# Attention and routed experts in one kernel: the remaining logits on VectorE, phase 0's last sum moved, a second bank for one turning, and a copied register

## The chip, the cores and the metric

The kernel runs as one program on one core of a Trainium2 chip. The metric is its time on the device in microseconds. Before the change three runs took 688.2, 688.75 and 691.17 us; the median is 688.75.

## The reference

The first half is attention with a window: 8 batches, 8 heads, 576 positions, 64 columns a head, all in float32. The second half sends each of the 4608 resulting rows `x` (512 columns) to one of 8 experts, by an assignment that is greedy over all rows and experts at once:

```
logits = x @ w_gate
for idx in argsort(-logits.flatten()):
    tok, e = idx // 8, idx % 8
    if assigned[tok] >= 0 or counts[e] >= 576: continue
    assigned[tok] = e; counts[e] += 1
for e in range(8):
    out[assigned == e] = relu(x[assigned == e] @ w1[e]) @ w2[e]
```

Each expert gets exactly 576 rows. `w1` has 512 x 1024 and `w2` 1024 x 512 elements an expert.

## The kernel before, in words

**Attention** fills about the first 203 us and leaves `x` in DRAM and the logits in SBUF (`L_sb`, 128 partitions, 8 experts, 36 columns).

**The router** (class `Router`) doesn't sort. It works in phases 0 to 7, and each phase settles one expert, the one that fills up next: it finds by counting which rows are its members, lists their numbers, and takes the expert and its rows out of the logits. In `few` (line 966) VectorE writes indicators `ind`, TensorE counts them (line 611), VectorE turns the counts to flags `sat` (line 625), and TensorE sums these over partitions (line 628). Then `T1` marks the members (line 911), `totals` (line 865) gives the counts `Dc` and the expert's key `mx`, `members` (line 708) makes `m`, its running sum `run` and the exclusive sum `ex` (lines 712 to 716), and TensorE makes positions of `ex` (line 723). From these come `loOH` (line 750), the small matmuls of line 759, and the row numbers `idx`. `later` (line 938) writes the logits that remain, `L1`: a penalty for full experts is added (`L2`), and another for the members. In phases 0 and 1 VectorE does that with two operations; from phase 2 on GpSimd does it with three (lines 949, 954, 955). The next phase's first choice reads `L1` (line 514).

**The experts** (class `MoE`) are computed one after the other, expert k beside the router's work on the next ones. SyncE reads the expert's number from SBUF into a register (`value_load`, line 1069) and loads its weights in pieces of 512 KB into four buffers `raw`. ScalarE casts each to a high part (line 1084) and VectorE subtracts to get the low part (line 1090). GpSimd gathers the expert's rows, five tiles `g`, with indirect DMAs (line 1106). Each tile is turned by `flip` (line 1116): four transposes by TensorE into one PSUM bank, a cast to `xh` by ScalarE, and `under`, VectorE's subtraction that gives `xl`. The bank of pool `ps_g` is the only one there; the last turnings of the first expert may use pool `ps_o`. Pool `ps_h` has four banks, for layer 1's sums. Layer 1 (line 1155) and layer 2 (lines 1199 to 1202) take three products of high and low parts. GpSimd scatters the results to `out` (line 1211).

**What sets the order.** In `first_expert` and in layer 2 of the first expert the engines TensorE, VectorE and ScalarE are wrapped in `OrderedCore` (line 470): they run in the order in which the program is written. There the generator `phase0` stands for the router, and each `go()` runs it to its next `yield`. Line 467 is the wrapper's, so that all instructions of that part carry it. `keep_warm(n)` (line 1111) issues `n` matmuls of zeros, 128 x 512, that nothing reads. Their numbers are in `ZEROS` and, inside `phase0`, in `ZEROS_0`. Around the end of phase 0 `first_expert` reads as below; the first `go()` is the last count, `go(2)` the flags `sat` and their sum, and the last one goes from `sel` over the members to their positions:

```
    m.low(W[0], raw[0], 1)
    go()
    a0 = m.flip(*ga[0], "o")
    m.keep_warm(ZEROS[2])
    go(2)
    m.low(W[1], raw[1], 0)
    a1 = m.flip(*ga[1])
    m.keep_warm(ZEROS[3])
    go()
```

In layer 2 of the first expert a counter `i` goes through the steps, and at `i` in `TURN_2` the next tile of the second expert is turned. From layer 1 of the second expert on, a planner at compile time orders each engine's instructions: among those that its own model of the times takes to be ready, it picks by the program's order. So an engine can have instructions in its queue that the program writes much later, and once queued they are run strictly in that order. `W_LOAD` and `W_SPLIT` say at which step a piece of weights is asked for and split. `m.marked` (line 1075) makes a copy of a register tile on VectorE; a load that reads the copy can't start before it. It is used for some loads of the first two experts.

Of the kernel before, what the change touches and what calls it, by code (L numbers as in the profile page):

```python
# [5 lines left out]
F32 = mybir.dt.float32  # L6
# [4 lines left out]
ALU = mybir.AluOpType  # L11
# [8 lines left out]
NT = N // 128  # L20
# [5 lines left out]
def attention(tc, pools, qk_in, v_in, rel_in, C, x_dram, L_sb, router):  # L26
# [292 lines left out]
    for n in range(NPAIRS + LAG + 2):  # L319
# [16 lines left out]
        if turns:  # L336
            ps = {}
            for t in (2, 1, 3):
                ps[t] = bank()
                turn(k, t, ps[t])  # L340
            turned(k, 2, ps[2], nc.scalar.copy)
# [15 lines left out]
        if turns:  # L357
            ps = bank()
            turn(k, 0, ps)
        if n < NPAIRS:  # L360
            scores(n, 0)
        if turns:
            turn(k, 4, ps)
            turned(k, 0, ps, nc.scalar.copy)
# [55 lines left out]
CONST_AT = 4  # L420
WARM, WARM0, WARM1 = 11, 16, 4
AHEAD = 18, 24, 24
ZEROS = 2, 4, 2, 3, 3
ZEROS_0 = 10, 2, 5, 8
CHOICE_1 = 1, 4
HIGHS_2 = 0, 3, 4, 5
LOWS_2 = 0, 0, 0, 2, 1, 2, 2, 1
# [3 lines left out]
CHOICE_2 = 25, 27, 31  # L431
SPLIT_2 = 26, 29
LATE_2 = 34
TURN_2 = 34, 36, 39
TURN_1, SPLIT_1, WAIT_1, SPLIT_W2, FLAGS_1 = (1, 2), (5, 6), 3, 8, 6
W_LOAD = [(0, 1, 0, 0), (0, 1, 1, 2), (0, 1, 2, 6), (0, 1, 3, 10),
          (1, 0, 0, 13), (1, 0, 1, 16), (1, 0, 2, 19), (1, 0, 3, 22), (1, 1, 0, 28)]
# [5 lines left out]
BIG = 1e30  # L443
# [12 lines left out]
def bc(ap, shape):  # L456
    return ap.to_broadcast(shape)
# [17 lines left out]
class Router:  # L475
# [462 lines left out]
    def later(self, k, L, T1, Dc, keyv, mx):  # L938

        nc, rt = self.nc, self.p["rt"]  # L940
        if k < 7:
            self.pen = self.small("pen", 8)
            nc.vector.tensor_scalar(self.pen, Dc, float(CAP), -BIG, ALU.is_ge, ALU.mult)
            self.base = self.small("base", 8)
            nc.vector.tensor_tensor(self.base, self.pen, Dc, ALU.add)
            nc.vector.scalar_tensor_tensor(self.left, keyv, mx[:, 0:1], self.left, ALU.not_equal, ALU.mult)
            L2 = rt.tile([128, 8, NT], F32, name="L2", bufs=1)
            eng = nc.vector if k < 2 else self.tc.nc.gpsimd
            eng.tensor_tensor(L2, L, bc(self.pen.unsqueeze(2), [128, 8, NT]), ALU.add)
            if k < 2:  # L950
                nc.vector.scalar_tensor_tensor(self.L1, T1, 100.0 * BIG, L2, ALU.mult, ALU.add)
            else:
                Lt = rt.tile([128, 8, NT], F32, name="Lt", bufs=1)
                eng.tensor_scalar(Lt, T1, 100.0 * BIG, 1.0, ALU.mult, ALU.mult)
                eng.tensor_tensor(self.L1, Lt, L2, ALU.add)

    def excess(self, Dc, mx):

# [102 lines left out]
class MoE:  # L1061
# [54 lines left out]
    def flip(self, h, g, r, pool="g"):  # L1116

        if h == 0:
            self.xg = [self.p["xg"].tile([128, 4, CAP], F32R, name=name) for name in ("xh", "xl")]
        if pool == "g":  # L1120
            ps = self.p["ps_g"].tile([128, 4, 128], F32, name="pg")
        else:
            ps = self.p["ps_o"].tile([128, 512], F32, name="po").rearrange("p (j t) -> p j t", j=4)
        for j in range(4):
            self.nc.tensor.transpose(ps[:, j, :r], g[:r, 128 * j:128 * j + 128], self.C["ident"][:r, :r])  # L1125
        self.nc.scalar.copy(self.xg[0][:, :, 128 * h:128 * h + r], ps[:, :, :r])  # L1126
        return h, r, ps
# [3 lines left out]
        xh, xl = (x[:, :, 128 * h:128 * h + r] for x in self.xg)  # L1131
        return self.nc.vector.tensor_tensor(xl, ps[:, :, :r], xh.bitcast(F32), ALU.subtract)  # L1132

    def turn(self, gs):

        for h, g, r in gs:
            yield self.under(*self.flip(h, g, r))

    def hidden(self):

# [121 lines left out]
def first_expert(tc, P, C, r, m, route):  # L1262

    nc = tc.nc
    r.nc = core = OrderedCore(tc)
    core.sync = nc.sync
    m.nc = core
    m.idle = P["ps_g"].tile([128, 512], F32, name="pg")
    p = r.phase0(lambda i: m.keep_warm(ZEROS_0[i]))

    def go(n=1):
        for _ in range(n):
            next(p)

    def ask(reg, layer, cs):
        return list(m.loads(reg, layer, cs))

    def marked(i):
        return m.marked(r.guess, i)

    cut = 0, AHEAD_ROWS, 576
    pp = {}

    def layer(f, t):
        for _ in m.steps1(W, f, cut, (t,), f < 2 and t == 0):
            pass
        pp[f, t] = m.pp

    def rest(f, t):
        m.rest1(pp[f, t], f, cut, (t,))  # L1290

    go()
    raw = ask(r.guess, 0, range(3))
    rows = [r.few_rows[:, t:t + 1] for t in range(2)]
    ga = m.gather(rows, range(2), m.x[0:128 * AHEAD_COLS, :])
    m.idle = P["ps_h"].tile([128, 512], F32, name="ph")
    W = [m.high(raw[c]) for c in range(2)]
    go(2)
    m.keep_warm(ZEROS[0])
    go(2)  # L1300
    m.low(W[0], raw[0], 0)
    m.keep_warm(ZEROS[1])
    go()
    m.low(W[0], raw[0], 1)
    go()
    a0 = m.flip(*ga[0], "o")
    m.keep_warm(ZEROS[2])
    go(2)
    m.low(W[1], raw[1], 0)
    a1 = m.flip(*ga[1])  # L1310
    m.keep_warm(ZEROS[3])
    go()
    m.under(*a0)
    m.under(*a1)
    late = marked(0)
    raw += ask(late, 0, (3,))
    second = ask(late, 1, (0,))
    m.keep_warm(ZEROS[4])
    m.hidden()
    go()  # L1320
    layer(0, 0)
    m.low(W[1], raw[1], 1)
    layer(1, 0)
    W.append(m.high(raw[2]))
    go()
    gb = m.gather(r.idx[0], range(2, 5))
    rest(0, 0)
    go()
    for half in range(2):
        m.low(W[2], raw[2], half)  # L1330
    layer(2, 0)
    W.append(m.high(raw[3]))
    rest(1, 0)
    layer(3, 0)
    go()
    rest(2, 0)
    layer(4, 0)
    for half in range(2):
        m.low(W[3], raw[3], half)
    rest(3, 0)  # L1340
    layer(5, 0)
    rest(4, 0)
    b = m.flip(*gb[0], "o")
    m.under(*b)
    late = marked(1)
    second += ask(late, 1, range(1, 4))
    layer(6, 0)
    rest(5, 0)
    b = [m.flip(*gb[1], "o"), m.flip(*gb[2])]
    m.under(*b[0])  # L1350
    rest(6, 0)
    m.under(*b[1])
    layer(7, 0)
    rest(7, 0)
    V, lows = [], []
    for f in range(8):
        layer(f, 1)
        if f == 0:
            go()
        if f in HIGHS_2:  # L1360
            V.append(m.high(second[len(V)]))
            lows += [(V[-1], second[len(V) - 1], half) for half in range(2)]
        if f:
            rest(f - 1, 1)
        if f in CHOICE_1:
            next(route)
        for _ in range(LOWS_2[f]):
            m.low(*lows.pop(0))
    rest(7, 1)
    next(route)  # L1370
    return V, p


def layer_moe(tc, P, C, r, m, exact):
    nc = tc.nc
    route = (n for k in range(1, E) for n in r.phase(k, exact))
    st = dict(wait=0, turn=0)
    raws, loaders, gathers = {}, {}, {}
    W = {}

    def load(e, layer):
        if (e, layer) not in loaders:
            loaders[e, layer] = m.loads(r.ei[e], layer)
            raws[e, layer], W[e, layer] = [], []
        raws[e, layer].append(next(loaders[e, layer]))

    def part(e, layer):
        W[e, layer].append(m.split(raws[e, layer][len(W[e, layer])]))
# [34 lines left out]
    if exact:  # L1423
        r.start(True)
        W[0, 0] = [m.split(raw) for raw in m.loads(r.ei[0], 0)]
        for _ in m.turn(m.gather(r.idx[0])):
            pass
        for _ in m.layer1(W.pop((0, 0))):
            pass
        V = [m.split(raw) for raw in m.loads(r.ei[0], 1)]  # L1430
        while 1 not in r.idx:
            next(route)
    else:
        V, p = first_expert(tc, P, C, r, m, route)
    i = 0
    for _ in m.layer2(V, m.h, r.idx[0], fine=True):
        i += 1
        if i in ROUTE_2 + CHOICE_2 and not exact:
            next(route)
        if i == ROUTE_2[-1]:  # L1440
            gathers[0] = m.turn(m.gather(r.idx[1]))
        if i == LOAD_2:
            raws[1, 0], W[1, 0] = list(m.loads(r.ei[1], 0, range(2))), []
        if i in SPLIT_2:
            part(1, 0)
        if i in TURN_2:
            turned = next(gathers[0])
        if i == LATE_2:
            late = m.marked(r.ei[1], 2)
            raws[1, 0] += m.loads(late, 0, (2, 3))  # L1450
            loaders[1, 1] = m.loads(late, 1)
            raws[1, 1], W[1, 1] = [], []
        if i == TURN_2[-1] and not exact:
            next(route)
# [55 lines left out]
def moe_attn_kernel(tc, qk, v, w1, w2, wn, rel, ident, cst, out):  # L1510
    nc = tc.nc
    with ExitStack() as es:
# [24 lines left out]
        for k, b in (("ps_g", 1), ("ps_h", 4), ("ps_o", 2)):  # L1537
            P[k] = es.enter_context(tc.tile_pool(name=k, bufs=b, space=PSUM))
        layer_moe(tc, P, C, r, m, False)
        again = P["rs"].tile([1, 1], I32, name="again")  # L1540
        nc.vector.tensor_copy(again, r.flag[0:1, 0:1])
        go = nc.values_load(again[0:1, 0:1], min_val=0, max_val=1)
        with tc.If(go > 0):
            r.nc = m.nc = nc
            layer_moe(tc, P, C, r, m, True)
# [26 lines left out]
```

## Time and profile before

| | |
|---|---|
| Median of three runs | 688.75 us |
| Profiled execution | 690.12 us, its span 688.2 us |
| TensorE busy | 97% of the span, 7299 matmuls |
| VectorE, ScalarE, GpSimd busy | 67%, 48%, 22% |
| Mean granted TensorE clock | 0.993 of full |
| Chain that ended last | PE 86%, DVE 7%, ACT 2%, DMA 2% of the span |

In the profile PE is TensorE, PEld its weight loads, DVE VectorE, ACT ScalarE, POOL GpSimd and SP SyncE. The span goes from the first to the last instruction; the execution's time is 1.92 us longer, and the profiled execution was 1.37 us above the median. In a timeline, the number in square brackets is how long the engine was idle before the instruction, with what released it. A matmul's duration includes its way through the array, so that durations of successive ones overlap.

### The profile page before, as it was taken

The numbers are of one execution on the slowest core, as the hardware profiler recorded it, in microseconds if no ns is written. First come the engines' busy times: TensorE is split into PE (matmuls) and PEld (weight loads), VectorE is DVE, ScalarE is ACT, GpSimd is POOL, SyncE is SP. The second block draws the span as 40 slices with busy tenths as digits, with TensorE's granted clock in tenths as the row PEclk, the third lists the DMA queues.
The fourth block names the chain that finished last, engine by engine and source line by source line (L and its number), as shares of the span: only waits on it lengthen the run. The fifth ranks groups of instructions, "written<-read, shape, count | busy, mean of one in ns | idle before, by whom it ended". The sixth has DMA issues, their size and how long they took to land.

```text
span 688.2 us, 18927 instructions
## 1 busy us (share of the span) xinstructions
PE 666.3 (97%) x7299; PEld 581.9 (85%) x7299; DVE 459.0 (67%) x1888; ACT 327.8 (48%) x992; POOL 149.4 (22%) x334
## 2 busy tenths in 40 slices
PE   8999999999996999999999999999999999999996
PEld 5899889989983996898798889879979988988985
DVE  6678888887878786799579377566746937423210
ACT  6898998898862441344414323322522524322201
POOL 4022222222121101304102311411311323111011
PEclk9999999999999999999999999999999999999999
DMA  8466575757324402626404503611810546401001
GB/s 297 156 199 214 183 232 172 217 179 227 119 86 147 156 36 93 222 70 217 158 9 158 201 25 123 208 47 31 290 48 24 184 162 199 155 31 38 1 25 50
DMA packets 35139, 92.72 MB, mean 135 GB/s; under 512 B 3808, under 2 KB 13152, under 8 KB 35040
## 3 DMA queue, kind: packets, MB, share of 16 engines
q1 hardware_dynamic: 29152, 72.55, 31.8%
q0 software_dynamic: 5888, 18.88, 8.4%
q8 instruction: 59, 0.97, 0.6%
q14 instruction: 40, 0.33, 0.2%
HBM read 72.54 MB, written 18.87 MB: 133 GB/s over the span
## 4 chain that ended last, share of the span: by engine, by line
PE 86%; DVE 7%; ACT 2%; DMA 2%; issue 1%; POOL 0%; POOLq 0%; SPq 0%; DVEq 0%; ACTq 0%
PE ph L1155 25%; PE po L1199 9%; PE po L1200 8%; PE pt L53 7%; PE po L1202 7%; PE x L53 6%; PE s L53 6%; PE pt L160 6%; PE ph L467 4%; PE po L467 2%; PE pg L1125 2%; ACT u L147 2%; DMA raw<-in_w_dram 1%; DMA g<-x,idxa 1%; PE x L1507 1%
## 5 line engine op out<-in xcount | busy, mean ns | idle before, releaser
L1155 PE MATMUL ph<-xh,hl 128*128 128x288 f32 x896 | 166.2, 299 | 0.0
L1155 PEld LDWEIGHTS ph<-xh,hl 128*128 128x128 f32 x896 | 134.6, 188 | 1.2 <-DVE hlo L1171 0.4
L147 ACT ACTIVATE u<-u,mn 128x192 f32<-128x192 f32 (+2 forms) x288 | 124.1, 439 | 5.5 <-DVE mn L137 5.4
L1199 PE MATMUL po<-hl,hh 128*128 128x512 f32 (+1 forms) x288 | 114.9, 399 | 0.0
L1200 PE MATMUL po<-hl,hh 128*128 128x512 f32 (+1 forms) x288 | 110.8, 385 | 0.0
L1155 PE MATMUL ph<-xl,hl 128*128 128x288 f32 x448 | 99.1, 296 | 0.0
L1160 ACT ACTIVATE hh<-ph 128x288 fp32r<-128x288 f32 x112 | 40.5, 408 | 120.0 <-PE ph L1155 117.8
L137 DVE CUSTOM_DVE_ANT_0 u<-s,bm 128x192 f32<-128x192 f32 (+1 forms) x248 | 71.8, 345 | 32.0 <-PE s L53 31.5
L1202 PE MATMUL po<-hl,hlo 128*128 128x512 f32 (+1 forms) x232 | 89.0, 384 | 0.0
L1211 POOL DMA_INDIRECT out_dram<-o,idx x38 | 41.4, 1090 | 204.5 <-ACT o L1206 81.2
L1090 DVE TENSOR_TENSOR hl<-raw,hl 128x512 fp32r<-128x512 f32 x108 | 70.5, 684 | 12.9 <-ACT hl L1084 12.3
L1084 ACT CAST hl<-raw 128x1024 fp32r<-128x1024 f32 x54 | 56.2, 1050 | 40.6 <-DMA raw<-in_w_dram 35.4
L1155 PEld LDWEIGHTS ph<-xl,hl 128*128 128x128 f32 x448 | 73.1, 188 | 0.1
L1199 PEld LDWEIGHTS po<-hl,hh 128*128 128x128 f32 x288 | 54.2, 188 | 10.1 <-issue 0.6
L1171 DVE SCALAR_TENSOR_TENSOR hlo<-ph,hh 128x288 fp32r<-128x288 f32 (+1 forms) x112 | 42.6, 416 | 29.5 <-ACT hh L1160 26.7
L1200 PEld LDWEIGHTS po<-hl,hh 128*128 128x128 f32 x288 | 54.3, 189 | 9.1
L53 PE MATMUL s<-qk 64*64 64x192 f32 (+1 forms) x992 | 60.6, 328 | 0.4 <-DVE mn L137 0.3
L1132 DVE TENSOR_TENSOR xl<-pg,xh 128x512 fp32r<-128x512 f32 (+1 forms) x32 | 20.2, 631 | 57.9 <-ACT xh L1126 57.8
L147 ACT ACTIVATION_READ_ACCUMULATOR u<-u,mn 128x1 f32 x288 | 56.3, 195 | 0.0
L1106 POOL DMA_INDIRECT g<-x,idx x38 | 40.4, 1063 | 68.4 <-issue 47.2
L160 PE MATMUL pt<-ident_sb,u 128*128 128x128 f32 x368 | 53.0, 280 | 0.5 <-ACT u L147 0.4
L1202 PEld LDWEIGHTS po<-hl,hlo 128*128 128x128 f32 x232 | 43.6, 188 | 8.9
(310 smaller groups left out, 1092.9 us busy)
## 6 DMA issues: line engine op xcount, KB each, us to landing
raw<-in_w_dram SPq DMA_DIRECT2D x64, 512.0 KB, 4.0
qk<-in_qk_dram SPq DMA_DIRECT2D x32, 576.0 KB, 5.6
v<-in_v_dram SPq DMA_DIRECT2D x32, 288.0 KB, 3.0
x<-xb SPq DMA_DIRECT2D x14, 512.0 KB, 4.1
x<-xb SPq DMA_DIRECT2D x8, 128.0 KB, 3.4
x<-xb SPq DMA_DIRECT2D x4, 256.0 KB
g<-x,idx POOLq DMA_INDIRECT x38, 6.2
out_dram<-o,idx POOLq DMA_INDIRECT x38, 2.7
```

The costliest lines, as they stand in the source:

```text
L53: put(nc.tensor.matmul(out, w, a, start=start, stop=stop, skip_group_check=True))
L137: put(nc.vector.tensor_tensor_reduce(out=weights(n, t, h), in0=x[:, c:c + 64 * m].rearrange("q (j k) -> q j k", k=64), in1=bm[n % NP][:, y ...
L147: put(nc.scalar.activation(u, u, AF.Exp, bias=st["mn"][:, i:i + 1], scale=-1.0, accum_out=st["sm"][:, i:i + 1]))
L160: put(nc.tensor.transpose(ps[:, c:c + 128], u[:, o + 128 * j:o + 128 * j + 128], ident))
L1084: self.nc.scalar.copy(hl[:, 0, :], raw)
L1090: self.nc.vector.tensor_tensor(hl[:, 1, c:c + 512], raw[:, c:c + 512], hl[:, 0, c:c + 512].bitcast(F32), ALU.subtract)
L1155: self.nc.tensor.matmul(pp[t], w[:, a, j, fo:fo + 128], x[:, j, cut[t]:cut[t + 1]], start=(i == 0), stop=(i == 11))
L1171: self.nc.vector.scalar_tensor_tensor(d, pp[t][:, c0:c1], 0.0, o[:, c0:c1].bitcast(F32), ALU.max, ALU.subtract)
L1199: nc.tensor.matmul(out, a, wh, start=(f == 0), stop=False)
L1200: nc.tensor.matmul(out, a, wl, start=False, stop=(f == 7 and t == 4))
L1202: nc.tensor.matmul(out, hl[:, f, 128 * t:128 * t + 128], wh, start=False, stop=(f == 7))
L1211: self.sent = self.tc.nc.gpsimd.indirect_dma_start(out=self.out, out_offset=bass.IndirectOffsetOnAxis(ap=idx[t][:r], axis=0), in_=o[:r, :] ...
```

## The change

`later` uses VectorE's two operations in all phases. In `first_expert`, the last count's flags and their sum come ahead of both turnings, and the numbers of fillers change. The second expert's second tile is turned through a bank of `ps_h`, and its third tile one step sooner. The loads of layer 2 of the third expert read a copied register.

```
-ZEROS = 2, 4, 2, 3, 3
-ZEROS_0 = 10, 2, 5, 8
+ZEROS = 2, 8, 3, 1, 1
+ZEROS_0 = 14, 2, 5, 9
-TURN_2 = 34, 36, 39
+TURN_2 = 34, 36, 38
...
-            eng = nc.vector if k < 2 else self.tc.nc.gpsimd
-            eng.tensor_tensor(L2, L, bc(self.pen.unsqueeze(2), [128, 8, NT]), ALU.add)
-            if k < 2:
-                nc.vector.scalar_tensor_tensor(self.L1, T1, 100.0 * BIG, L2, ALU.mult, ALU.add)
-            else:
-                Lt = rt.tile([128, 8, NT], F32, name="Lt", bufs=1)
-                eng.tensor_scalar(Lt, T1, 100.0 * BIG, 1.0, ALU.mult, ALU.mult)
-                eng.tensor_tensor(self.L1, Lt, L2, ALU.add)
+            nc.vector.tensor_tensor(L2, L, bc(self.pen.unsqueeze(2), [128, 8, NT]), ALU.add)
+            nc.vector.scalar_tensor_tensor(self.L1, T1, 100.0 * BIG, L2, ALU.mult, ALU.add)
...
-        if pool == "g":
-            ps = self.p["ps_g"].tile([128, 4, 128], F32, name="pg")
-        else:
-            ps = self.p["ps_o"].tile([128, 512], F32, name="po").rearrange("p (j t) -> p j t", j=4)
+        ps = self.p["ps_" + pool].tile([128, 512], F32, name="p" + pool).rearrange("p (j t) -> p j t", j=4)
...
-    def turn(self, gs):
+    def turn(self, gs, pools="ggggg"):
...
-            yield self.under(*self.flip(h, g, r))
+            yield self.under(*self.flip(h, g, r, pools[h]))
...
+    m.keep_warm(ZEROS[2])
+    go()
+    m.low(W[1], raw[1], 0)
+    go()
     a0 = m.flip(*ga[0], "o")
-    m.keep_warm(ZEROS[2])
-    go(2)
-    m.low(W[1], raw[1], 0)
     a1 = m.flip(*ga[1])
     m.keep_warm(ZEROS[3])
     go()
...
-            loaders[e, layer] = m.loads(r.ei[e], layer)
+            loaders[e, layer] = m.loads(m.marked(r.ei[e], 3) if (e, layer) == (2, 1) else r.ei[e], layer)
...
-            gathers[0] = m.turn(m.gather(r.idx[1]))
+            gathers[0] = m.turn(m.gather(r.idx[1]), "ghggg")
```

## Rows read from the trace of the kernel before

**Rows 1.** The page, busy time of each engine: us (share of the span) x instructions.

```profile
PE 666.3 (97%) x7299; PEld 581.9 (85%) x7299; DVE 459.0 (67%) x1888; ACT 327.8 (48%) x992; POOL 149.4 (22%) x334
```

**Rows 2.** Timeline of PE, 219 to 228 us: start, duration, operation, [idle before].

```profile
220.33 0.66 PE L467 MATMUL po<-ident_sb,g 128*128 128x128 f32 x4 [0.61 <-DMA g<-x,idxa]
...
221.51 0.18 PE L467 MATMUL m<-sat,c_ones 64*128 64x1 bf16 x1
...
222.53 1.49 PE L467 MATMUL ph<-zero 128*128 128x512 bf16 x3
...
224.68 1.30 PE L467 MATMUL ph<-xh,hl 128*128 128x256 f32 x8
...
227.74 0.41 PE L467 MATMUL m<-mv,loOH 128*128 128x24 bf16 x10
```

**Rows 3.** Timeline of DVE, 219 to 228 us.

```profile
220.33 0.15 DVE L467 TENSOR_SCALAR sat<-mx 64x1 bf16<-64x1 f32 x1
...
221.73 0.25 DVE L467 TENSOR_SCALAR sel<-kq,m 128x36 bf16<-128x36 bf16 x1 [0.63 <-PE m L467]
...
225.47 1.42 DVE L467 TENSOR_TENSOR loOH<-c_i,slo 128x1152 bf16<-128x1152 bf16 x2
```

**Rows 4.** Windows of half a microsecond: PE, PEld, DVE, ACT, POOL, clock, DMA.

```profile
221.00:221.50 0.50, 0.50 (x2) 0.00 (x0) 0.10 (x1) 0.48 (x1) 0.00 (x0) 0.63 0.00 0
224.50:225.00 0.50, 0.50 (x5) 0.32 (x3) 0.43 (x3) 0.00 (x0) 0.00 (x0) 0.96 0.00 0
```

**Rows 5.** Timeline of all engines, 280 to 286 us.

```profile
281.47 0.69 DVE L467 TENSOR_TENSOR xl<-pg,xh 128x512 fp32r<-128x512 f32 x1 [0.87 <-issue]
...
282.22 0.66 PE L467 MATMUL pg<-ident_sb,g 128*128 128x128 f32 x4 [0.48 <-DVE late L467]
```

**Rows 6.** Timeline of all engines, 325 to 333 us.

```profile
329.43 1.05 ACT L1084 CAST hl<-raw 128x1024 fp32r<-128x1024 f32 x1 [2.45 <-DMA raw<-in_w_dram]
...
332.23 0.66 PE L1125 MATMUL pg<-ident_sb,g 128*128 128x128 f32 x4 [1.22 <-DVE xl L1132]
```

**Rows 7.** Timeline of SP, 320 to 330 us: loads issued, with count.

```profile
321.01 5.04 SPq L1072 DMA_DIRECT2D raw<-in_w_dram  x4
```

**Rows 8.** Timeline of all engines, 364.5 to 368 us, one of four such stretches.

```profile
365.23 0.67 POOL L949 TENSOR_TENSOR L<-L,pen 128x288 f32<-128x288 f32 x1 [1.91 <-DVE ov L961]
...
365.38 0.56 DVE L712 SCALAR_TENSOR_TENSOR m<-am,kmx,sel 128x36 bf16<-128x36 bf16 x1
...
365.97 0.85 POOL L955 TENSOR_TENSOR L<-Lt,L 128x288 f32<-128x288 f32 x1
...
366.06 0.85 DVE L714 TENSOR_TENSOR_SCAN run<-c_ones,m 128x36 bf16<-128x36 bf16 x1
...
367.67 0.19 PE L723 MATMUL m<-ex,c_ones 128*128 128x36 bf16 x1 [0.79 <-DVE ex L716]
```

**Rows 9.** Waits, whole run: us in total, times, longest.

```profile
PE m L467 <- DVE ind L467: 3.7, 4, 1.6
...
PE m L723 <- DVE ex L716: 3.2, 4, 0.8
```

**Rows 10.** Groups of DVE, phases 0 and 1: busy us, mean ns | idle before.

```profile
L467 DVE SCALAR_TENSOR_TENSOR L<-T,L 128x288 f32<-128x288 bf16 x2 | 0.9, 458 | 0.1
...
L467 DVE TENSOR_TENSOR_SCAN run<-c_ones,m 128x36 bf16<-128x36 bf16 (+1 forms) x3 | 0.7, 227 | 0.1
...
L467 DVE TENSOR_TENSOR L<-L,pen 128x288 f32<-128x288 f32 x1 | 0.5, 451 | 0.0
...
L467 DVE SCALAR_TENSOR_TENSOR m<-am,kmx,sel 128x36 bf16<-128x36 bf16 x1 | 0.2, 245 | 0.0
```

**Rows 11.** The page, costliest groups: the gathers of GpSimd.

```profile
L1106 POOL DMA_INDIRECT g<-x,idx x38 | 40.4, 1063 | 68.4 <-issue 47.2
```

**Rows 12.** Line 1090 on DVE: min/median/max ns, first and last start.

```profile
L1090 DVE TENSOR_TENSOR hl<-raw,hl x108: 670/681/736, 298.9 to 631.7; 128x512 fp32r<-128x512 f32 x108
```

**Rows 13.** Groups of PE, the fillers of phase 0.

```profile
L467 PE MATMUL pg<-zero 128*128 128x512 bf16 x25 | 6.1, 379 | 0.0
```

## The prediction, made before the changed kernel was run

> **What bounds the kernel now.** I read the page first: TensorE is busy for 666.3 of 688.2 us [rows 1]. So nothing is gained by making other engines faster as such. What can be gained is TensorE's waiting, of which there is 21.9 us in all, and the filler matmuls that keep it busy while it waits. The change touches four places, and I read the timeline at each.
>
> *Place A, the first expert's start (219 to 228 us).* TensorE works in the written order. The last count of phase 0 is followed by the first turning, which waits 0.61 us for its gathered rows, and by two fillers; only then, at 221.51, comes the small matmul that sums the flags `sat` [rows 2]. VectorE had `sat` ready at 220.33 + 0.15 = 220.48 [rows 3]. So the sum stands 1.03 us behind work that it doesn't need, and VectorE, which needs it for `sel`, sat idle 0.63 us before 221.73 [rows 3]. The granted clock also fell, to 0.63 of full in the half microsecond from 221.0, which is the change from 2.4 to 1.2 GHz inside that slice, and was back at 0.96 in the slice from 224.5 [rows 4]. Three fillers at that lower level took 1.49 us, and layer 1 began at 224.68 [rows 2].
>
> *Place B, the second expert's turnings (280 to 286).* The turning at 282.22 waits 0.48 us, since the one transposition bank is read until VectorE's subtraction at 281.47 (0.69 us) is through [rows 5].
>
> *Place C, the third expert's turnings (325 to 333).* ScalarE's queue holds a weight cast at 329.43 that waited 2.45 us for its transfer; the cast of the turned rows stands behind it, and TensorE's next turning, at 332.23, waits 1.22 us for the bank [rows 6]. The four loads of that expert's second layer were issued from 321.01 on, while the gathers were in flight [rows 7].
>
> *Place D, four later phases.* GpSimd adds up the new logits just while VectorE makes the list of chosen tokens. Here `m` (0.56 us) and the running sum (0.85 us) end within 0.1 us after GpSimd's two additions end, and TensorE waits 0.79 us for what follows [rows 8]. This wait comes four times, 3.2 us together [rows 9]. The same two VectorE operations take 0.245 and 0.227 us where GpSimd is not adding [rows 10]. So 0.31 + 0.62 = 0.93 us per phase is the price of the two engines meeting, more than the whole wait.
>
> **The change part by part.** *D: the logits on VectorE.* Five phases (2 to 6) lose three GpSimd operations and gain two of VectorE, 0.451 + 0.458 = 0.91 us as phases 0 and 1 show them [rows 10]. In four of the phases VectorE gets back 0.93 us, so its load is nearly even. The question is where the planner puts the two. Behind the list of tokens, the list is done 0.93 us sooner and 3.2 us of waiting go. Ahead of it, the gain is 0.93 - 0.91 = 0.02 us a phase, unless the planner, which then sees VectorE occupied, also moves TensorE's matmul back. Either order that the planner foresees hides the wait, because what it did not foresee was the meeting of the engines. I take 2.7 of 3.2 us, with 0.1 and 3.2 as bounds. Phase 2 shows no such wait; its added 0.91 us I cost at nothing, since TensorE has layer 1 to do beside it, and at 0.9 us if that cover is gone.
>
> The page "SBUF — State Buffer" of the Trainium skill, section "Who interferes with whom", has a rule against this part: a VectorE operation with two inputs in SBUF and a GpSimd operation that reads SBUF exclude each other, and the later one blocks for the whole of the other.
>
> GpSimd still issues gathers and scatters, a gather about 1.06 us [rows 11]. If one held up the moved additions, up to 1.06 us a phase would come back, 4.2 us in four phases, and D would gain nothing. Against it: VectorE's weight subtraction, also with two inputs in SBUF, ran 108 times from 299 to 632 us, between 0.670 and 0.736 us [rows 12], with gathers and scatters all along. I cost it at nothing.
>
> *A: the last sum ahead of the turnings.* The sum now follows `sat` directly, at about 220.5. VectorE has one weight subtraction of 0.69 us in between, so `sel` starts at about 221.1 instead of 221.73, 0.63 us sooner. The two turnings (eight transposes and two ScalarE casts, no DMA) follow the sum; the first one's rows are there at 220.33 [rows 2], and the second one's were asked for right behind them. Of the six fillers behind the sum, three and three, one and one are left. At the full clock layer 1 can begin at about 222.7, 2.0 us sooner. But the next list's matmul, now at 227.74, needs `loOH`, which ends at 225.47 + 1.42 = 226.89 and comes 0.63 us sooner, 226.26 [rows 2, 3]. Layer 1's 3.06 us up to there give 222.7 + 3.06 = 225.8, so TensorE waits 0.5 us and goes on at about 226.3: a gain of 1.45 us. If the clock falls as before, some 1.2 us of layer 1 run at half rate, and the gain is 0.8. The bounds are 0.8 and 2.0.
>
> *Fillers added.* Four, one and four more stand in phase 0, and one more behind the last count. Each takes about 0.24 us [rows 13], a group of four 0.98 us. They stand ahead of matmuls that wait for VectorE's `ind`, 3.7 us in four waits, the longest 1.6 [rows 9], so I cost them at nothing; where a wait is shorter than the group put into it, the rest is lost, 0.98 us at most for one group. Whether they hold the clock can't be seen in the trace of before; that is why A keeps both ends.
>
> *B: the idle bank.* The second turning writes a bank of layer 1's own pool, which nothing uses then; 0.48 us of waiting goes. The third turning still needs the first bank, which is free by 282.2, and comes one step sooner, so that the casts for layer 1 are in time. I take 0.45 us; bounds 0 and 0.5.
>
> *C: the copied register.* One copy on VectorE (about 0.13 us) is added, and SyncE waits for it before it loads layer 2 of the third expert. Behind that wait stand these four loads and then the next expert's. The planner now sees the weights later, and should place their casts behind the turned rows' casts. The gathers also get the DMA engines to themselves for longer. I take 1.0 of 1.22 us. The upper bound is 1.2; below nothing is treated under the rivals.
>
> *Sum.* 2.7 + 1.45 + 0.45 + 1.0 = 5.6 us. Outside these places TensorE hardly waits between 228 us and the tail, so nothing there absorbs a gain. The profiled execution took 690.12 us with a span of 688.2, so it would take 684.5. The median of the three runs shown, 688.75, is 1.37 us below it, and I forecast 683.2.
>
> **Rivals.** *1. The stalls at D stay.* The two additions get ahead of the list, and TensorE's matmul keeps its place. Then D gives 0.1 us and the rest 2.9: 685.75. For it: the planner fills every gap in that chain with whatever is ready. Against it: the planner weighs VectorE's own time, and it was only the meeting that it missed. The rule of the Trainium skill above, were it to hold for gathers, would lead to this same time; I give it no more than 0.02 of this chance.
>
> *2. The change at C does nothing.* The register is known long before 321 us. If the planner puts the copy early, the loads go out as now, the cast keeps its place and 1.0 us is not gained: 684.2.
>
> *3. Slower: the cast keeps its place and its weights come later.* If the loads start later than 321.01 but ScalarE's order stays, the cast at 329.43 holds the turned rows longer, one for one. From 4.6 us on (loads from 325.6), this takes more than the 4.6 us that A, B and D give. With loads from about 328 the price is 7 us: 688.75 - 4.6 + 7 = 691.2. For it: the copy has no urgent place. Against it: the planner knows of the copy.
>
> **How the numbers follow.** The forecast has 0.46, and its own range is 681.4 to 684.9. The first rival has 0.24 (684.6 to 687), the second 0.16 (683 to 685.5), the third 0.14 (688 to 695). A difference of 0.5%, 3.44 us, is about what a measurement of this kernel can tell from no change, so the lines are 685.3 and 692.2. Faster by that: all but a trace of the forecast, 0.44, a quarter of the first rival, 0.07, and nearly all of the second, 0.14, 0.65 in all. Slower: half of the third, 0.07. The rest, 0.28, is no difference. The range, 681.5 to 688.0, leaves out the third rival and a little of the forecast's low end.
>
> **What would show it.** Right: the sum of `sat` right behind its count and fillers; layer 1 of the first expert from about 222.7 on; no wait at the second expert's second turning; the turned rows' cast ahead of the weight cast at 330; `m` and the running sum near 0.25 us in all phases; no 0.8 us wait before the list's matmul; GpSimd without additions after 205 us. Wrong: the clock at 1.2 GHz inside layer 1; a ScalarE cast waiting for `raw` ahead of a turning; waits for `ex` still there; new waits of TensorE for VectorE in phases 2 to 6.

## The result, and the profile after

The changed kernel takes 682.86 us (median of 6, 681.91 to 683.49), where the kernel before takes 688.48 beside it: a ratio of 0.9912 (95% interval 0.9893 to 0.9931; here and below the ratio is estimated from all runs, so that it can differ a little from that of the medians). Run again with the last experiments it gave 682.86 once more, a ratio of 0.9900 (0.9884 to 0.9916). The forecast was 683.2. The profiled execution took 682.88 us with a span of 681.1.

First the page, busy time of each engine (compare [rows 1]).

```profile
PE 663.9 (97%) x7303; PEld 580.2 (85%) x7305; DVE 459.0 (67%) x1899; ACT 326.2 (48%) x992; POOL 140.4 (21%) x319
```

TensorE's idle time fell from 21.9 to 17.2 us. VectorE took over ten operations and is as busy as before, since two others of it got shorter (place D).

**Place A.** The timeline of TensorE from the last count to the next list's matmul (compare [rows 2]):

```profile
217.77 0.69 PE L467 MATMUL m<-OH,ind 128*128 128x16 bf16 x18
218.29 0.81 PE L467 MATMUL ph<-zero 128*128 128x512 bf16 x3
219.10 0.17 PE L467 MATMUL m<-sat,c_ones 64*128 64x1 bf16 x1
219.52 0.63 PE L467 MATMUL po<-ident_sb,g 128*128 128x128 f32 x4 [0.25 <-issue]
...
221.32 1.21 PE L467 MATMUL ph<-xh,hl 128*128 128x256 f32 x8
...
224.86 0.39 PE L467 MATMUL m<-mv,loOH 128*128 128x24 bf16 x9 [0.42 <-ACT hh L467]
```

VectorE beside it (compare [rows 3]):

```profile
218.90 0.15 DVE L467 TENSOR_SCALAR sat<-mx 64x1 bf16<-64x1 f32 x1
219.59 0.24 DVE L467 TENSOR_SCALAR sel<-kq,m 128x36 bf16<-128x36 bf16 x1
223.32 1.42 DVE L467 TENSOR_TENSOR loOH<-c_i,slo 128x1152 bf16<-128x1152 bf16 x2
```

The sum follows `sat` by 0.20 us instead of 1.18, `sel` by 0.69 instead of 1.40. From the start of `sat` layer 1 begins 2.42 us later (before: 4.35) and the list's matmul 5.96 us later (before: 7.41). That is 1.45 us less, with the order and the fillers changed together. The granted clock fell too, but earlier: it was at 0.50 from 213.9 on, through most of the eight fillers ahead of the last count, and back at 1.00 before the turnings (windows, columns as in [rows 4]):

```profile
214.00:214.50 0.50, 0.38 (x1) 0.00 (x0) 0.43 (x4) 0.00 (x0) 0.50 (x1) 0.50 0.61 197
...
217.50:218.00 0.50, 0.50 (x11) 0.33 (x10) 0.50 (x2) 0.00 (x0) 0.00 (x0) 1.00 0.69 262
```

**Place B.** The second expert's turnings, first before, then after (timelines of TensorE; one line of before is in [rows 5]):

```profile
280.21 0.60 PE L467 MATMUL pg<-ident_sb,g 128*128 128x128 f32 x4
...
285.74 1.21 PE L1155 MATMUL ph<-xh,hl 128*128 128x288 f32 x8
```

```profile
277.32 0.60 PE L467 MATMUL pg<-ident_sb,g 128*128 128x128 f32 x4
278.69 0.60 PE L467 MATMUL ph<-ident_sb,g 128*128 128x128 f32 x4
...
281.94 1.22 PE L1146 MATMUL ph<-xh,hl 128*128 128x288 f32 x8
```

From the first turning to layer 1 it was 5.53 us and is 4.62 us, 0.91 less, though the recorded wait was only 0.48. Where TensorE doesn't wait, a matmul here mostly starts 0.16 us ahead of the recorded end of the one before it (in place D of the changed kernel at 361.96, against 362.12), so each gap costs 0.16 us more than its recorded idle time. Before had two gaps here (0.48 and 0.01), 0.81 us together; the rest of the 0.91 is not explained.

**Place C.** ScalarE and TensorE at the third expert's turnings (compare [rows 6]):

```profile
323.44 0.59 ACT L1117 CAST xh<-pg 128x512 fp32r<-128x512 f32 x1
...
327.29 0.60 PE L1116 MATMUL pg<-ident_sb,g 128*128 128x128 f32 x4
327.42 1.05 ACT L1078 CAST hl<-raw 128x1024 fp32r<-128x1024 f32 x1 [3.39 <-DMA raw<-in_w_dram]
328.37 0.58 ACT L1117 CAST xh<-pg 128x512 fp32r<-128x512 f32 x1
```

The first turned rows' cast now stands ahead of the weight cast that waits 3.39 us for its transfer, and the next turning does not wait. From the list of phase 2 (here and from now on the matmul that takes `ex`, line 723) to the fourth turning it was 28.43 us and is 27.27, 1.16 less.

**Place D.** Phase 3's list again, first one more line of before, then after (compare [rows 8]):

```profile
366.88 0.64 DVE L514 TENSOR_REDUCE b<-L 128x36 f32<-128x288 f32 x1
```

```profile
360.38 0.45 DVE L948 TENSOR_TENSOR L<-L,pen 128x288 f32<-128x288 f32 x1
...
360.81 0.24 DVE L712 SCALAR_TENSOR_TENSOR m<-am,kmx,sel 128x36 bf16<-128x36 bf16 x1
...
361.17 0.22 DVE L714 TENSOR_TENSOR_SCAN run<-c_ones,m 128x36 bf16<-128x36 bf16 x1
361.32 0.43 DVE L949 SCALAR_TENSOR_TENSOR L<-T,L 128x288 f32<-128x288 bf16 x1
361.67 0.17 DVE L716 TENSOR_TENSOR ex<-run,m 128x36 bf16<-128x36 bf16 x1
361.82 0.67 DVE L514 TENSOR_REDUCE b<-L 128x36 f32<-128x288 f32 x1
361.96 0.19 PE L723 MATMUL m<-ex,c_ones 128*128 128x36 bf16 x1
```

Both additions went ahead of `ex`, and still `ex` starts 1.58 us after `pen`, where it was 2.47. The stalls gave back 0.93 us, and the additions cost the list next to nothing, since they took the place of the next phase's first choice (line 514): that stood ahead of `ex` before and stands behind it now. It is so in all four phases. None of the six phases has a wait for `ex`. From the third expert's fourth turning to the last list it was 230.12 us and is 226.88, 3.24 less. Phase 2's two additions cost nothing: from the second expert's layer 1 to its list it took 26.42 us before and 26.38 after.

One wait is new, at the second turning of the fourth expert, where a weight cast that waited 2.38 us for its transfer stands ahead of the turned rows' cast, as in place C before:

```profile
380.73 0.66 PE L1116 MATMUL pg<-ident_sb,g 128*128 128x128 f32 x4 [0.28 <-DVE xl L1123]
```

From phase 3's list to phase 4's it got 0.48 us shorter, while the next two phases got 0.94 and 1.02 shorter. Of the profiles with one bank at that turning, all seven with the additions on VectorE have such a wait (0.22 to 1.05 us), and none of the five with them on GpSimd.

The four places give 1.45 + 0.91 + 1.16 + 3.24 = 6.76 us in this pair of profiles. TensorE's last matmul came 8.8 us sooner. Most of the difference is no part of the change: `sat` itself came 1.4 us sooner (1.7 us from before's clock, which fell during attention, 0.82 between 20 and 25 us, less 0.3 us that the stretch of the added fillers took longer), and 0.6 us arose in one expert's layer 1. The end after the last matmul was 1.7 us longer.

### The profile page after: what moved, and what is told of

It is laid out like the page before. It is cut to its first block, busy times and chain, and to the rows that moved or that the text cites. A ratio compares the mean times of both kernels' runs of the same rounds, so it can differ in the third digit from the quotient of the medians.

```text
span 681.1 us, 18925 instructions
## 1 busy us (share of the span) xinstructions
PE 663.9 (97%) x7303; PEld 580.2 (85%) x7305; DVE 459.0 (67%) x1899; ACT 326.2 (48%) x992; POOL 140.4 (21%) x319
## 4 chain that ended last, share of the span: by engine, by line
PE 87%; DVE 7%; ACT 3%; DMA 1%; issue 1%; POOL 0%; POOLq 0%; SPq 0%; DVEq 0%; ACTq 0%
PE ph L1146 25%; PE po L1190 9%; PE po L1191 8%; PE po L1193 7%; PE pt L53 7%; PE x L53 6%; PE s L53 6%; PE pt L160 6%; PE ph L467 4%; PE po L467 3%; ACT u L147 2%; PE pg L1116 2%; DVE hl L1084 1%; PE m L467 1%; DMA raw<-in_w_dram 1%
## 5 line engine op out<-in xcount | busy, mean ns | idle before, releaser
L1084 DVE TENSOR_TENSOR hl<-raw,hl 128x512 fp32r<-128x512 f32 x108 | 69.6, 683 | 17.3 <-ACT hl L1078 17.2
```

The lines of the kernel that those rows point to most:

```text
L1084: self.nc.vector.tensor_tensor(hl[:, 1, c:c + 512], raw[:, c:c + 512], hl[:, 0, c:c + 512].bitcast(F32), ALU.subtract)
```

## The experiments

Four kernels do one part alone. Line numbers of a part's own kernel differ a little.

**D alone.** Before, with `later`'s GpSimd branch replaced:

```
+            nc.vector.tensor_tensor(L2, L, bc(self.pen.unsqueeze(2), [128, 8, NT]), ALU.add)
+            nc.vector.scalar_tensor_tensor(self.L1, T1, 100.0 * BIG, L2, ALU.mult, ALU.add)
```

> Before, with the remaining logits on VectorE in all phases and nothing else. Theory (VectorE's list operations were held by GpSimd's additions): m near 0.245 us and the running sum near 0.225 us in all six phases, no wait of TensorE for ex, and 3.2 us less (2.8 to 3.5), a ratio of 0.9953. Rival (the two additions get ahead of the list and cost what the meeting cost): waits for ex stay, 0 to 0.5 us less.

Measured: 685.26 us against 688.83, a ratio of 0.9950 (0.9932 to 0.9968), 3.6 us less. `m` and the running sum in all six phases (min/median/max, ns):

```profile
L712 DVE SCALAR_TENSOR_TENSOR m<-am,kmx,sel x6: 246/248/249, 309.0 to 561.4; 128x36 bf16<-128x36 bf16 x6
L714 DVE TENSOR_TENSOR_SCAN run<-c_ones,m x6: 224/226/228, 309.8 to 561.7; 128x36 bf16<-128x36 bf16 x6
```

No wait for `ex` is left. This is the largest part, somewhat over the sum of the waits. In this profile the third expert's turnings have no wait either, and the fourth's have the new one, 0.97 us.

**A alone.** Before, with the new order and the new fillers.

```
+ZEROS = 2, 8, 3, 1, 1
+ZEROS_0 = 14, 2, 5, 9
...
+    m.keep_warm(ZEROS[2])
+    go()
+    m.low(W[1], raw[1], 0)
+    go()
     a0 = m.flip(*ga[0], "o")
```

> Before, with the order of phase 0's last sum and the new numbers of fillers, nothing else. Theory (the sum stood behind work that it did not need): from sat to the list's matmul 5.9 to 6.0 us where before has 7.4, and 1.45 us less in all (0.8 to 2.0). Rival (the fillers, through the clock, give the gain or take it back): the stretch gets shorter, but fillers at half rate ahead of the last count cost up to 1 us and 0.5 us or less remains.

Measured: 687.46 against 688.83, 0.998 (0.9966 to 0.9994), 1.4 us less. From `sat` (219.12) to the list's matmul:

```profile
225.09 0.62 PE L467 MATMUL m<-mv,loOH 128*128 128x24 bf16 x18 [0.41 <-ACT hh L467]
```

That is 5.97 us, as in the changed kernel. The other three places stay much as they were (the third expert's wait is 0.82 us), the waits for `ex` included.

**B alone.** Before, with `turn(..., "ghggg")` for the second expert and `TURN_2 = 34, 36, 38`.

> Before, with the second turning of the second expert through a bank of layer 1's pool and the third one step sooner, nothing else. Theory (the wait and TensorE's draining and refilling around it go): from the first turning to layer 1 of the second expert 4.6 us instead of 5.5, 0.9 us less in all. Rival (only the recorded wait goes): 0.45 us less.

Measured: 688.17 against 688.83, 0.9986 (0.9972 to 1.0000), 0.7 us less. The turnings:

```profile
278.63 0.60 PE L467 MATMUL pg<-ident_sb,g 128*128 128x128 f32 x4
...
283.22 1.22 PE L1152 MATMUL ph<-xh,hl 128*128 128x288 f32 x8
```

4.59 us, 0.94 less than before in the same stretch, so the theory's 0.9 and not the recorded 0.48.

**C alone.** Before, with `m.loads(m.marked(r.ei[e], 3) ...)` for layer 2 of the third expert.

> Before, with the copied register ahead of the loads of the third expert's second layer, nothing else. Theory (the planner puts the turned rows' cast ahead of one weight cast): no wait of about 1.2 us ahead of the third expert's second turning, 1.15 us less in all (0.9 to 1.3). Rival (the copy is early, the cast keeps its place): 0. Rival (it needs the other parts to get the order right): less than 0.5 us, with the wait at another turning.

Measured: 687.89 against 688.83, 0.9989 (0.9972 to 1.0007). The median is 0.9 us lower, but the interval includes no change, and the twelve runs went from 685.2 to 691.9, wider than in any other kernel here. The profile is of the slowest of them; ScalarE, VectorE and TensorE in its timeline:

```profile
327.74 0.13 DVE L1078 COPY late<-ei 1x1 int32<-1x1 int32 x1
...
332.47 1.05 ACT L1084 CAST hl<-raw 128x1024 fp32r<-128x1024 f32 x1 [4.49 <-DMA raw<-in_w_dram]
334.81 1.05 ACT L1084 CAST hl<-raw 128x1024 fp32r<-128x1024 f32 x1 [1.29 <-DMA raw<-in_w_dram]
335.76 0.58 ACT L1126 CAST xh<-pg 128x512 fp32r<-128x512 f32 x1
...
337.24 0.66 PE L1125 MATMUL pg<-ident_sb,g 128*128 128x128 f32 x4 [1.97 <-DVE xl L1132]
```

The copy came 1.07 us after the first turning (in the changed kernel 0.26 us ahead of it), since it stood behind work of VectorE that waited for weights. The transfers came late, two weight casts held up the second turned rows' cast, and the wait grew to 1.97 us at the third turning. In this one execution the weights came late, as in the prediction's third rival; but the first turned rows' cast did go ahead, and the wait moved to another turning. The same profile had the clock at 0.50 from 215.1 to 225.3, in place A, and from 337.9 to 341.4, behind the long wait, so that its 691.9 us are not the wait's alone.

**The changed kernel without C.**

> The changed kernel without the copied register: the loads of the third expert's second layer read the register as before. Theory (the copy is what brings the turned rows' cast ahead): a wait of TensorE of 0.8 to 1.3 us at the third expert's turnings comes back, and the time is about 683.8 us, 0.9 us above the changed kernel. Rival (with the logits on VectorE the turnings come out without a wait already, as they did when that part was done alone): 682.9, the same within 0.3 us.

Measured: 683.77 us (682.88 to 688.11), against 682.86: 0.9 us, as the theory has it, though the intervals overlap (0.9905 to 0.9936 of before, beside 0.9893 to 0.9931), so that it could be nothing. The profile is of the run with 688.11:

```profile
328.24 1.04 ACT L1078 CAST hl<-raw 128x1024 fp32r<-128x1024 f32 x1 [2.66 <-DMA raw<-in_w_dram]
329.67 0.59 ACT L1117 CAST xh<-pg 128x512 fp32r<-128x512 f32 x1
331.04 1.12 PE L1116 MATMUL pg<-ident_sb,g 128*128 128x128 f32 x4 [2.79 <-DVE xl L1123]
```

Behind this wait the granted clock was at its lower level, 1.2 GHz (one window, columns as in [rows 4]):

```profile
331.00:334.00 3.00, 2.96 (x9) 2.58 (x10) 1.27 (x2) 0.59 (x1) 0.43 (x1) 0.50 0.23 87
```

It came back at 334.4. At half the rate for 3.4 us TensorE lost, by estimate, some 1.7 us more than the wait; the 4.5 us together are about what sets this run apart from the other five (682.9 to 684.1).

Over all profiles with one bank at the third expert, the wait (0.8 us or more) came in four of six without the copy (before, A, B, this one; not with D alone or the fillers alone) and in two of six with it. Six and six profiles are too few to say that the copy makes it rarer. In all six that have it, the wait came behind a weight cast that waited for its transfer.

**Idle additions on GpSimd**, to find out why D works: the changed kernel, and after the two additions on VectorE

```
+            if k > 1:
+                Lt = rt.tile([128, 8, NT], F32, name="Lt", bufs=1)
+                pool = self.tc.nc.gpsimd
+                pool.tensor_tensor(Lt, T1, bc(self.pen.unsqueeze(2), [128, 8, NT]), ALU.add)
+                pool.tensor_tensor(Lt, Lt, bc(self.pen.unsqueeze(2), [128, 8, NT]), ALU.add)
```

> The changed kernel, with two additions on GpSimd in phases 2 to 6 (128 x 288, T1 plus pen, then that plus pen) whose results nothing reads; the order of TensorE, VectorE and ScalarE is that of the changed kernel. Theory (the two engines hold each other up when both read SBUF): m or the running sum, or the two moved operations, take 0.3 to 0.6 us longer where they meet an addition, TensorE waits for ex again in four or five phases, 0.8 to 1.7 us each, and the time is 3 to 7 us above the changed kernel's 682.9. Rival (what cost the time was the list's dependence on GpSimd's sum, or its place in the order): nothing waits for the new operations, so 682.9 within 0.5 us and m at 0.245 us.

Measured: 685.56 us, 0.9950 (0.9933 to 0.9967) of before, 2.7 us above the changed kernel. Phase 3's list in its timeline:

```profile
362.07 0.95 POOL L953 TENSOR_TENSOR Lt<-T,pen 128x288 f32<-128x288 bf16 x1 [16.04 <-DVE kmx L874]
...
362.47 0.60 DVE L712 SCALAR_TENSOR_TENSOR m<-am,kmx,sel 128x36 bf16<-128x36 bf16 x1
...
363.10 0.70 POOL L954 TENSOR_TENSOR Lt<-Lt,pen 128x288 f32<-128x288 f32 x1
...
363.19 0.70 DVE L714 TENSOR_TENSOR_SCAN run<-c_ones,m 128x36 bf16<-128x36 bf16 x1
```

Nothing reads these sums, and still `m` ends at 363.07 and the running sum at 363.89, each within 0.1 us after a GpSimd operation's end, as in [rows 8]. TensorE waits again, 0.61 us in each of four phases, 2.4 in all. So the meeting of the two engines costs time by itself, with no dependence on GpSimd's result. GpSimd's first addition took 0.95 us, beside 0.67 in phase 2; it began 0.04 us behind VectorE's two-input addition at 362.03, so the later one of the two waits, whichever it is.

**Idle operations with one tensor input**: as the kernel above, with `pool.tensor_scalar(Lt, T1, self.pen[:, 0:1], 1.0, ALU.mult, ALU.mult)`, and a second one that has `Lt` for `T1`.

> As the kernel with two idle additions on GpSimd, but with two operations of one tensor input and a scalar per partition (128 x 288) in their place. Theory (any GpSimd operation that reads SBUF holds the two-input operations of VectorE): m and the running sum are long again where they meet them, and the time is 2 to 6 us above 682.9. Rival (only GpSimd's two-input operations do it): m near 0.245 and the running sum near 0.225 us, 682.9 within 0.5 us.

Measured: 683.73 us, 0.9924 (0.9905 to 0.9942), 0.9 above the changed kernel. The timeline of the same list:

```profile
361.77 0.77 POOL L953 TENSOR_SCALAR Lt<-T,pen 128x288 f32<-128x288 bf16 x1 [16.07 <-DVE kmx L874]
...
362.14 0.44 DVE L712 SCALAR_TENSOR_TENSOR m<-am,kmx,sel 128x36 bf16<-128x36 bf16 x1
...
362.64 0.55 POOL L954 TENSOR_SCALAR Lt<-Lt,pen 128x288 f32<-128x288 f32 x1
362.70 0.22 DVE L714 TENSOR_TENSOR_SCAN run<-c_ones,m 128x36 bf16<-128x36 bf16 x1
362.84 0.65 DVE L949 SCALAR_TENSOR_TENSOR L<-T,L 128x288 f32<-128x288 bf16 x1
```

`m` again ends right behind GpSimd's operation (362.58 against 362.54), and the moved addition takes 0.65 us instead of 0.43. But the running sum ran through beside the second operation at 0.22 us. The two began 0.06 us apart, and GpSimd's took 0.55 us, where the one-input operation of line 954 took 0.43 alone in before; it may be GpSimd that waited there. So one-input operations hold VectorE too, shorter; whether any two-input operation of VectorE is free of it isn't shown. The waits for the list come to 0.7 us in the four phases; the profile also has 1.49 us at the third expert's turnings, and in the medians 0.9 us is no clear difference, since the intervals overlap.

**The old fillers in the changed kernel** (`ZEROS` and `ZEROS_0` of before, the new order kept).

> The changed kernel with the numbers of fillers of before (10, 2, 5, 8 in phase 0; 2, 4, 2, 3, 3 around its last sums). Theory (the order gives the gain of place A and the added fillers cost and bring nothing, except that five fillers more stand behind the sum): from sat to the list's matmul 5.9 to 6.3 us, and the time 682.9 to 683.4 us. Rival (the fillers hold the clock through the turnings and the start of layer 1): the granted clock is 0.5 inside that stretch, it takes 6.8 us or more, and the time is 683.7 or more.

Measured: 682.87 us (682.25 to 684.91), the changed kernel's median, as the theory has it. But the profile, of the slowest of the six runs (another took 684.7, the other four at most 682.9), has the stretch at 7.25 us, with the clock at 0.50 in it:

```profile
220.59 0.18 PE L467 MATMUL m<-sat,c_ones 64*128 64x1 bf16 x1
222.74 1.45 PE L467 MATMUL ph<-zero 128*128 128x512 bf16 x3
...
227.63 0.54 PE L467 MATMUL m<-mv,loOH 128*128 128x24 bf16 x15
```

`sel` came 0.69 us after `sat`, as in the changed kernel. Then the turnings ran at half rate, their casts held VectorE's subtractions for 0.5 us, and `loOH` was late again, as the rival has it.

**The new fillers alone**, in the kernel before, with the old order.

> Before, with the new numbers of fillers alone, the last sum still behind the first turning. Theory (the fillers bring the clock's fall ahead of the turnings, and the order brings the rest): from sat to the list's matmul 6.6 to 7.0 us, and 0 to 0.5 us less than before. Rival (they are pure cost, since they stand ahead of matmuls that VectorE has already released): 0.5 to 1.5 us more than before.

Measured: 688.75 against 689.74, 0.9987 (0.9973 to 1.0002). From `sat` (219.01) to the list's matmul:

```profile
219.62 0.17 PE L467 MATMUL m<-sat,c_ones 64*128 64x1 bf16 x1
...
225.12 0.61 PE L467 MATMUL m<-mv,loOH 128*128 128x24 bf16 x18 [0.50 <-DVE off L467]
```

6.11 us, with the clock at full from 217.5 on; shorter than either theory had. So in the profiles the fillers alone shorten the stretch by 1.3 us, the order alone by 0.16, and both by 1.45. The other profiles say the same: in all nine with the new fillers the clock was back at full by 219.3 and the stretch took at most 6.11 us, and in all five with the old ones the clock was at 0.50 inside it and it took 6.80 to 8.08 us. What each is worth in the median isn't settled: the fillers alone show 1.0 us beside their own runs of before, and the old fillers lost nothing in the kernel above. The runs of one kernel spread by more than that.

**A second bank in all turnings.** The changed kernel with `m.turn(m.gather(r.idx[k + 1]), "ghghg")` in `slot`, once with and once without C, and the changed kernel again beside them.

> The changed kernel itself, run beside the three that follow. Both theories: 682.9 us within 0.5; from sat to the list's matmul 5.9 to 6.0 us; no wait for ex; TensorE's wait at the third expert's turnings between 0 and 1.5 us, since it hangs on when the weights land.

> The changed kernel with every later expert's second and fourth turning through a bank of layer 1's pool, too. Theory (what TensorE waits for at the turnings is the one bank, which a late weight cast ahead of the turned rows' cast keeps full): no wait for xl at any turning, whenever the weights land, 0.3 to 0.8 us below the changed kernel. Rival (the wait goes over to layer 1's first matmul, or layer 1 waits for its own bank): the same within 0.3 us, with new waits of TensorE at layer 1.

> As the kernel with a second bank in all turnings, but without the copied register. Theory of the bank: the copy is no longer needed, the time is that of the kernel with both, within 0.3 us. Rival (the transfers' order is what counts at the third expert): 0.9 us above it, with a wait of TensorE at the third expert's turnings.

Measured: 682.86 (the changed kernel), 682.91 with the banks, ratio 0.9895 (0.9875 to 0.9915), and 682.43 with the banks and without C, the same ratio. TensorE's waits from 300 us on: the changed kernel has one, at the fourth expert's turnings, and with the banks the list is empty, with or without C.

```profile
PE pg L1116 <- DVE xl L1123: 1.0, 1, 1.0
```

At the fourth expert a weight cast came late with the banks too (378.39, after 2.65 us of waiting for its transfer, ahead of the turned rows' cast at 379.34), and the second turning, at 380.71, did not wait. So it is the single bank that turns a late cast into a wait, and in these runs the copy is not needed beside the banks. But the gain of 0.45 to 1.2 us that the profiles show from phase 3's list to phase 4's (53.69 us with the banks, 54.14 and 54.91 in the two profiles of the changed kernel) doesn't rise above the spread of the runs (680.6 to 683.7 and 681.2 to 684.8). No version here is measurably faster than the changed kernel.

## Why the prediction was right, and where it was off

The sum was 5.6 us; the medians show 5.6 and, beside the last experiments, 6.9. The parts alone give 3.6, 1.4, 0.7 and 0.9 us by their medians, 6.5 together (for the last two the intervals reach to no change), so they add up within the spread of the runs: gains at four places of one chain of TensorE. That was the forecast's reason. That nothing after them absorbs a gain held but for the fourth expert's new wait, one of the signs of being wrong that the prediction names. The sum came out near in part because its terms erred both ways: D, B and C were taken too small, and A, with its fillers, somewhat too large.

- **D**: predicted 2.7 with 3.2 as the upper bound, measured 3.24 in the profile and 3.6 alone. The reason was right, and the two idle-work kernels show it. The upper bound was mis-sized: I summed the idle times in [rows 9], but a wait of 0.79 us costs 0.16 us more than its idle time (place B), 0.95 us; two phases got 0.94 and 1.02 us shorter. The step on the order was wrong as well: both additions went ahead of `ex`, where the prediction had only 0.02 us left to gain (rival 1's condition). The gain stayed, since the next phase's first choice went behind `ex` in their place.
- **The rule** of the Trainium skill (page "SBUF — State Buffer", section "Who interferes with whom"), that a two-input VectorE operation and a GpSimd operation that reads SBUF exclude each other, agrees with `m` at 0.60 us and the running sum at 0.70 beside idle additions. Read as a rule for gathers, it would have cost the gain. That was hardly put to the test: in the changed kernel's profile no gather ran beside the additions of phases 2 to 6 (0.43 to 0.46 us each). In phase 1 an addition of VectorE that began inside a gather of 1.02 us took 0.46 us.
- **A**: predicted 1.45 for the stretch, measured 1.45, with layer 1 1.93 us sooner (predicted 2.0) and a wait of 0.42 us at the list (predicted 0.5). That the number fits is luck, for its reason failed: I put the gain on the order, costed the added fillers at nothing and left open whether they hold the clock. In the profiles the order alone gives 0.16 us, below the 0.8 that I had for a fallen clock, and the fillers alone 1.3. The clock fell ahead of the group of eight fillers and was back before the turnings, which so ran at 2.4 GHz. In return the first list's matmul came 7.66 us ahead of `sat` instead of 7.37: the fillers cost 0.3 us, and A is worth some 1.15 us in this profile. Of the nine profiles with the new fillers, both in which the clock didn't fall have 7.32 us there, the others 7.37 to 7.93; so at the full clock the cost of nothing was right.
- **B**: predicted 0.45, measured 0.91. Again I took the recorded wait for the whole; the two gaps there cost 0.16 us more each.
- **C**: predicted 1.0, measured 1.16 in the profile and, within the spread of the runs, 0.9 by leaving it out. One weight cast moved, not all. The wait was also gone without the copy (D alone, the fillers alone), and came with it, longer, where the copy was late (C alone), which is near to rivals 2 and 3. When the weights land differs between executions, and I had treated it as fixed by the order.
- **Phase 2's additions**, costed at nothing, cost nothing.

## What to carry to other kernels

Where two engines' operations end within 0.1 us of each other several times over, compare their durations with a place where they don't meet; an idle copy of the work on the other engine shows whether it is the meeting that costs. A wait on the bounding engine can cost more than its recorded idle time: here 0.91 us for 0.48, 0.94 to 1.02 for 0.79, though not at place C (1.16 for 1.22); and behind a wait of 2.79 us the clock was at half for 3.4 us more. A wait behind a transfer should be read from several executions, since here it ranged from none to 2.8 us between kernels that differed little at that place, and in the two profiles with a second buffer it was gone, while with the order of casts alone it came in two of six.

## What was unexpected of the hardware

In twelve of the fourteen profiles the granted clock fell to 0.50, which is 1.2 GHz, in phase 0, first at 208 to 221 us; in the changed kernel at 213.9, behind idle gaps of TensorE of 0.55 and 0.78 us. With the new order and fillers the stretch from `sat` to the list's matmul took 5.96 to 6.06 us in eight profiles, whatever the clock had done ahead of it (in two of them it hadn't fallen). Why it fell at such different times stays open.

In one expert's layer 1 all 192 matmuls kept a pitch of 130.0 ns instead of 133.3 in some executions (24.96 us in the changed kernel's profile, 25.60 before), at a granted clock of 1.00 in both. The end of the span lay 5.8 to 7.8 us behind the end of TensorE's last matmul, both of them in executions of the changed kernel. Neither was looked into.
